# Scores and maxima of an attention kernel in 32-row tiles of TensorE, with the MLP run by token block between them

## The chip, the cores and the metric

The kernel runs on one core of one Trainium2 chip. The metric is the device time of one execution in microseconds. Before the change the median of 3 runs is 1124.44 us (1124.19 to 1124.58).

## The reference

One sequence of 2048 tokens, width 448, 16 heads of 28. Keys and values have one head, which all 16 query heads share. Attention and a two-layer MLP (hidden width 1792) both work on the normalized input, and both are added to it:

```python
xn = _layernorm(x, axis=-1)
# attention: one k and one v for all heads
q = (xn @ wq).reshape(B, S, H, Dh).transpose(0, 2, 1, 3)
k = xn @ wk
v = xn @ wv
scores = jnp.einsum("bhqd,bkd->bhqk", q, k) * (Dh ** -0.5)
o = jnp.einsum("bhqk,bkd->bhqd", _softmax(scores), v)
# result
x + o.transpose(0, 2, 1, 3).reshape(B, S, H * Dh) @ wo + jnp.maximum(xn @ w1, 0) @ w2
```

## The kernel before, in words

Matmuls that must be exact to float32 are made of single-pass float32r matmuls on parts: a value is split into a high part (rounded to float32r) and a low part (the rest), and high x high, high x low and low x high are summed in PSUM.

**Front.** x is loaded, normalized (`moments`, `rstd`, `normalized_x`), and transposed on PE (`transposed`, L222) into `xH`, `xL`, `xR`, which stay on chip. For each of four blocks of 512 tokens, `qkv_proj` (L252, L168, L173) makes four groups of columns: four heads each, with a part of k or v beside them. `qkv_out` splits each result (L235, L236) and stores high and low part to `qscr` in DRAM (L237).

**MLP.** It follows at once, before the attention. `tasks` runs over 7 parts of 256 hidden columns, and inside a part over the 4 token blocks. `mlp_up` makes two tiles of 11 matmuls (L168, L173), ACT applies the ReLU (L391), DVE makes the low part `hL` (L392). `mlp_down` makes four tiles of 6 matmuls (L404), which DVE adds into `acc` (L411). Each part's weights are loaded and split once (`split_part` on POOL, L147 and L148). Four of the 28 tasks also carry row maxima, 192 tiles in all.

**Attention.** A unit is one block of 512 queries and one group of four heads; there are 16 units, each with 16 blocks of 128 keys. `load_stack` puts four copies of the query parts over one another on 112 rows (high, low, high, low), and `kst` holds the keys in the same way (high, high, low, low), so one full-height matmul makes an exact score. `max_tile` (L350) makes a tile of scores with queries as rows, and DVE reduces it to row maxima (L354): 64 tiles a unit. When a unit is done, `max_all` and `max_rows` bring the negated maxima into two more rows of the query stack (L371, L373, L377), and `score` (L628) makes the scores with keys as rows, 114 rows high, with the maximum already taken off; ACT applies the exponential (L630) into a tile `p`. `pv` multiplies four heads' `p` tiles by the values, each in 32 columns of the array (L474), and a column of ones gives the denominators. Then `dens`, `recips`, `normalized` and the output projection (L529, L550) follow, and `finish` closes the last unit (L571 to L589).

**What sets the order.** Every engine runs its instructions in program order. In the attention a list written out by hand, `ORDER`, sets it: S is a score, M a maximum tile, V and a number so many PV blocks, F an output projection. PSUM has three pools: `psA` with 3 banks, `psM` with 4, `psO` with 1. All loads and stores from the middle of the program are issued from one queue, SP, in program order.

Of the kernel before, what the change touches and what calls it, by code (L numbers as in the profile page):

```python
# [15 lines left out]

@with_exitstack
def attention_plus_mlp(ctx: ExitStack, tc: tile.TileContext, x, wq, wk, wv, wo, w1, w2, out):
    nc = tc.nc
    P = 128
# [4 lines left out]
    NT = S // P  # L29
    QB = 512  # L30
    NQB = S // QB
    TPB = QB // P
    HG = 4
    NHG = H // HG
    NKB = S // P
# [4 lines left out]
    NPART = DFF // FP  # L40
# [5 lines left out]
    KQ = 4 * DH  # L46
    NU = NQB * NHG
    NA, NM = 3, 4
    assert DR == 64 and KQ + 2 <= P and HG * 32 == P and NPART * FP == DFF
# [5 lines left out]
    psA = ctx.enter_context(tc.tile_pool(name="psA", bufs=NA, space=PSUM))  # L55
    psM = ctx.enter_context(tc.tile_pool(name="psM", bufs=NM, space=PSUM))
    psO = ctx.enter_context(tc.tile_pool(name="psO", bufs=1, space=PSUM))


    acc = cst.tile([P, NT, D], F32, name="acc")  # L60
    xv = x.rearrange("(t p) d -> p t d", p=P)
    for t in range(TPB):
        (nc.scalar if t % 2 else nc.sync).dma_start(acc[:, t, :], xv[:, t, :])

    ident = cst.tile([P, P], F32, name="ident")
    make_identity(nc, ident)
    vtile = cst.tile([P, NKB, 32], F32, name="vtile")
    nc.gpsimd.memset(vtile, 1.0)
    ones2 = cst.tile([2, QB], F32, name="ones2")
    nc.gpsimd.memset(ones2, 1.0)  # L70
    eps_t = cst.tile([P, 1], F32, name="eps_t")
    nc.vector.memset(eps_t, EPS)
    warm = cst.tile([P, 1], F32, name="warm")

# [3 lines left out]
    kst = cst.tile([P, S], F32R, name="kst")  # L78
    qscr = dram.tile([NHG, 2, P, S], F32, name="qscr")
    rscr = dram.tile([NU, HG, QB], F32, name="rscr")  # L80
    stacks = ctx.enter_context(tc.tile_pool(name="stacks", bufs=3))


    mlp = ExitStack()
    spool = mlp.enter_context(tc.tile_pool(name="spool", bufs=2))
    wpool = mlp.enter_context(tc.tile_pool(name="wpool", bufs=2))
    xpool = mlp.enter_context(tc.tile_pool(name="xpool", bufs=1))
    hpool = mlp.enter_context(tc.tile_pool(name="hpool", bufs=2))
    proj_scope = ExitStack()
    npool = proj_scope.enter_context(tc.tile_pool(name="npool", bufs=1, side="right"))  # L90
# [13 lines left out]
    DHH = DH // 2  # L104
    MQ = HG * DH
    stg = spool.tile([P, 2048], F32, name="stg")
    s3 = stg[:, 0 : (DC + 1) * D].rearrange("p (c n) -> p c n", c=DC + 1)
    kvs = stg[:, (DC + 1) * D : (DC + 1) * (D + 2 * DH)].rearrange("p (c n) -> p c n", c=DC + 1)
# [4 lines left out]
    wqkv = wpool.tile([P, 2, 4, 512], F32R, name="w")  # L113
    w4 = wqkv.rearrange("p s c (g n) -> p s c g n", g=NHG)
    nc.gpsimd.memset(w4[:, :, :, :, MQ + DHH : P].bitcast(F32), 0.0)
    for t in range(TPB, NT):
        nc.sync.dma_start(acc[:, t, :], xv[:, t, :])

    def wqkv_parts(c, kv):
        src = (kvs if kv else s3)[:, c].rearrange("p (g n) -> p g n", g=NHG)  # L120
        cols = slice(MQ, MQ + DHH) if kv else slice(0, MQ)
        return src, w4[:, 0, c, :, cols], w4[:, 1, c, :, cols]
# [9 lines left out]
    parts = {}  # L132

    def load_part(p):
        f0 = p * FP
        g = spool.tile([P, 2048], F32, name="stg")
        chunks_in(g[:, 0:W1C].rearrange("p (c n) -> p c n", c=DC + 1), w1[:, f0 : f0 + FP])
        nc.sync.dma_start(
            g[:, W1C : W1C + W2C].rearrange("p (c n) -> p c n", c=FC),
            w2[f0 : f0 + FP].rearrange("(c p) n -> p c n", p=P),  # L140
        )
        return g

    def split_part(p, g):
        n = W1C + W2C
        wt = wpool.tile([P, 2, 2048], F32R, name="w")
        nc.gpsimd.tensor_scalar(wt[:, 0, 0:n], g[:, 0:n], 1.0, 0.0, op0=ALU.mult, op1=ALU.add)  # L147
        nc.gpsimd.tensor_tensor(wt[:, 1, 0:n], g[:, 0:n], wt[:, 0, 0:n].bitcast(F32), op=ALU.subtract)  # L148
        parts[p] = (
            wt[:, :, 0:W1C].rearrange("p s (c n) -> p s c n", c=DC + 1),  # L150
            wt[:, :, W1C:n].rearrange("p s (c n) -> p s c n", c=FC),
        )


    xH = xpool.tile([P, DC, S], F32R, name="xH")
    xL = xpool.tile([P, DC, S], F32R, name="xL")
    xR = xpool.tile([P, S], F32R, name="xR")
    kstF = kst.bitcast(F32)

    def proj(ps, lhs, cols, xs, between=None, middle=None):  # L160

        n = 0
        for ws, xm in (((0, 1), xH), ((0,), xL)):
            if middle and xm is xL:
                middle()
            for c in range(DC):
                for wi in ws:
                    nc.tensor.matmul(ps, lhs[:, wi, c, cols], xm[:, c, xs], start=n == 0, stop=False)  # L168
                    n += 1
                    if between and n % 4 == 0:  # L170
                        between()
        for wi in range(2):
            nc.tensor.matmul(ps, lhs[:, wi, DC, cols], xR[:, xs], start=False, stop=wi == 1)  # L173
# [3 lines left out]
    def moments(b):  # L177
        mv = small.tile([P, TPB, 2], F32, name="mv")
        for i in range(TPB):
            st = small.tile([P, 6], F32, name="st")  # L180
            nc.vector.bn_stats(st, acc[:, b * TPB + i, :])  # L181
            nc.vector.bn_aggr(mv[:, i, :], st)
# [3 lines left out]

# [11 lines left out]
    def normalized_x(b, on_act=(1, 3)):  # L198

        mv, rs, nb = stat.pop(b)  # L200
        xn = []
        for i in range(TPB):
            if i % 2 == 0:
                pair = hpool.tile([P, FC, QB], F32, name="hL" if i else "hH")
            n = pair[:, i % 2]
            a = acc[:, b * TPB + i, :]
# [10 lines left out]
    def transposed(b, xn, chunks=range(DC + 1), order=range(TPB)):  # L217
        xs = slice(b * QB, (b + 1) * QB)
        for c in chunks:
# [3 lines left out]
            if c < DC:  # L223
                nc.scalar.activation(xH[:, c, xs], pt, AF.Copy)
                nc.vector.tensor_tensor(xL[:, c, xs], pt, xH[:, c, xs].bitcast(F32), op=ALU.subtract)
            else:
                tmp = small.tile([P, QB], F32R, name="tmp")
                nc.scalar.activation(xR[0:DR, xs], pt[0:DR], AF.Copy)
                nc.scalar.activation(tmp[DR:P], pt[DR:P], AF.Copy)
                nc.vector.tensor_tensor(xR[DR:P, xs], pt[DR:P], tmp[DR:P].bitcast(F32), op=ALU.subtract)  # L230
# [7 lines left out]

    def qkv_proj(b, g, spare=False, middle=None):
        pq = psO.tile([P, QB], F32, name="o") if spare else psA.tile([P, QB], F32, name="a")  # L240
        proj(pq, wqkv, slice(g * P, (g + 1) * P), slice(b * QB, (b + 1) * QB), middle=middle)
        return pq

    def qkv_first(gs):

        pq = [psA.tile([P, QB], F32, name="a") for _ in gs]
        passes = [(0, xH, c) for c in range(DC)] + [(0, xL, c) for c in range(DC)] + [(0, None, DC)]
        passes += [(1, xH, c) for c in range(DC)] + [(1, None, DC)]
        for n, (wi, xm, c) in enumerate(passes):
            for k, g in enumerate(gs):  # L250
                rhs = xR[:, 0:QB] if xm is None else xm[:, c, 0:QB]
                nc.tensor.matmul(  # L252
                    pq[k], wqkv[:, wi, c, g * P : (g + 1) * P], rhs, start=n == 0, stop=n == len(passes) - 1
                )
        return pq

# [18 lines left out]


# [5 lines left out]
    g0 = load_part(0)  # L282
    g1 = load_part(1)
    pq = qkv_proj(0, 3, spare=True, middle=lambda: transposed(1, xn))
    qkv_out(0, 3, pq)
    for b in range(1, NQB):
# [10 lines left out]
        qkv_out(b, 2, qkv_proj(b, 2))  # L297
        if b == 2:
            split_part(0, g0)
        pq = qkv_proj(b, 3, middle=None if last else lambda: transposed(b + 1, xn))  # L300
        qkv_out(b, 3, pq)
    proj_scope.close()
    stacks2 = ctx.enter_context(tc.tile_pool(name="stacks2", bufs=2, side="right"))


    for g in range(2):
        for r in range(4):
            d0 = r * DH + g * DHH
            nc.sync.dma_start(kstF[d0 : d0 + DHH, :], qscr[g, r // 2, MQ : MQ + DHH])
    for b in range(NQB):  # L310
        nc.sync.dma_start(kstF[KQ : KQ + 2, b * QB : (b + 1) * QB], ones2)
    vT = []
    for s in range(2):
        t = stacks.tile([P, HG, QB], F32, name="qst")
        vT.append(t.rearrange("d j q -> d (j q)")[0:DH])
        for g in range(2):
            nc.sync.dma_start(vT[s][g * DHH : (g + 1) * DHH], qscr[2 + g, s, MQ : MQ + DHH])
    nc.gpsimd.tensor_tensor(vT[0], vT[0], vT[1], op=ALU.add)

    def v_rows():  # L320

        pv = psM.tile([P, QB], F32, name="m")
        for kb in range(NKB):
            nc.tensor.transpose(pv[:, kb * 32 : kb * 32 + DH], vT[0][:, kb * P : (kb + 1) * P], ident[0:DH, 0:DH])
        nc.vector.tensor_copy(vtile[:, :, 0:DH], pv.rearrange("p (i d) -> p i d", d=32)[:, :, 0:DH])


    qst, nmx, mx_todo = {}, {}, []
    units = [(b, g) for b in range(NQB) for g in range(NHG)]

    def load_stack(u):
        if u >= NU:
            return
        b, g = units[u]
# [353 lines left out]
```

## Time and profile before

| | |
|---|---|
| median of 3 runs | 1124.44 us |
| span of the profiled execution | 1122.0 us |
| PE busy | 1116.4 us, 99% |
| DVE busy | 791.9 us, 71% |
| ACT busy | 588.5 us, 52% |
| POOL busy | 115.9 us, 10% |
| instructions | 15424 |
| DMA, mean over the span | 41 GB/s |

The span runs from the first instruction of the profiled execution to the last. PE is TensorE's matmuls, PEld its weight loads, DVE VectorE, ACT ScalarE, POOL GpSimd, SP the queue that issues DMAs. A group's row reads: line, engine, operation, output<-input by the program's names, shapes, count, then busy time, mean ns of one, and idle time before it with what ended it. A matmul in float32 (L474) shows two instructions for one call. A matmul's own length includes its way through the array, so neighbours overlap: what one costs in a stream is the distance between starts.

### The profile page before, as it was taken

To read this page: it belongs to the slowest core of one execution; us is meant where nothing else is said; L and a number is where in the kernel's file an instruction comes from. 1 tells how busy PE (TensorE), PEld (TensorE's weight loads), DVE (VectorE), ACT (ScalarE), POOL (GpSimd) and SP (SyncE) were. 2 spreads that over 40 slices of the span, in tenths; PEclk is the share of its full clock that TensorE was granted. 3 is DMA by queue.
4 is the path that set the end of the run, shared out by engine and by line. 5 is a ranking of instruction groups with operands and counts; after the bars stand their busy time and mean duration, and the time that the engine had idled before them with its cause. 6 is when DMAs were issued, how large, how long until landed. Compare 5 with 4: busy or idle time off the path is not lost.

```text
span 1122.0 us, 15424 instructions
## 1 busy us (share of the span) xinstructions
PE 1116.4 (99%) x5900; PEld 743.6 (66%) x5900; DVE 791.9 (71%) x1383; ACT 588.5 (52%) x1173; POOL 115.9 (10%) x100
## 2 busy tenths in 40 slices
PE   9999999999999999999999999999999999999998
PEld 8888888888888755555656555556565555656555
DVE  7634337888888878778876878876877877777602
ACT  5511110011000467767866767766766777666894
POOL 3232022020200101010010101101011010010110
PEclk9999999999999999999999999999999999999999
DMA  7781610001000101011012020111101100000001
GB/s 242 259 175 39 144 36 1 1 1 37 1 1 1 30 1 44 12 33 44 15 30 59 11 52 2 44 24 37 43 18 44 33 12 11 18 11 10 11 11 41
DMA packets 34432, 45.95 MB, mean 41 GB/s; under 512 B 10056, under 2 KB 21000, under 8 KB 34192
## 3 DMA queue, kind: packets, MB, share of 16 engines
q1 hardware_dynamic: 34072, 44.52, 15.1%
q8 instruction: 46, 0.75, 0.3%
q10 hardware_dynamic: 288, 0.46, 0.1%
q14 instruction: 26, 0.21, 0.1%
HBM read 32.37 MB, written 12.18 MB: 40 GB/s over the span
## 4 chain that ended last, share of the span: by engine, by line
PE 99%; DVE 0%; DMA 0%; issue 0%; ACT 0%
PE a L628 22%; PE m L350 22%; PE o L474 21%; PE a L168 12%; PE a L404 9%; PE o L404 3%; PE a L173 3%; PE m L529 3%; PE m L628 1%; PE m L550 1%; PE a L252 1%; PE m L222 1%; DMA acc<-in_A_x 0%; PE a L588 0%; DVE st L181 0%; PE o L168 0%
## 5 line engine op out<-in xcount | busy, mean ns | idle before, releaser
L354 DVE TENSOR_REDUCE nmx<-m 128x1 f32<-128x512 f32 x1024 | 633.0, 681 | 151.5 <-PE m L350 151.1
L630 ACT ACTIVATE p<-a 128x512 f32<-128x512 f32 x974 | 495.0, 638 | 163.9 <-PE a L628 163.2
L350 PE MATMUL m<-kst,qst 112*128 112x512 f32 x1024 | 393.4, 400 | 0.0
L628 PE MATMUL a<-qst,kst 114*128 114x512 f32 x974 | 379.5, 413 | 0.0
L628 PEld LDWEIGHTS a<-qst,kst 114*128 114x128 f32 x974 | 182.9, 188 | 139.6 <-ACT p L630 63.6
L474 PE MATMUL o<-p,vtile 128*32 128x512 f32 x2048 | 236.3, 596 | 0.0
L350 PEld LDWEIGHTS m<-kst,qst 112*128 112x128 f32 x1024 | 193.5, 189 | 42.1 <-DVE nmx L354 12.5
L391 ACT ACTIVATE hH<-a 128x512 fp32r<-128x512 f32 x56 | 33.5, 599 | 266.0 <-PE a L173 143.0
L474 PEld LDWEIGHTS o<-p,vtile 128*32 128x32 f32 x2048 | 58.5, 109 | 127.2 <-issue 123.0
L168 PE MATMUL a<-xH,w 128*128 128x512 f32 x408 | 110.0, 392 | 0.0
L404 PE MATMUL a<-w,hH 128*128 128x448 f32 x336 | 96.0, 367 | 0.0
L392 DVE SCALAR_TENSOR_TENSOR hL<-a,hH 128x512 fp32r<-128x512 f32 x56 | 38.7, 692 | 69.7 <-ACT hH L391 69.7
L168 PEld LDWEIGHTS a<-xH,w 128*128 128x128 f32 x408 | 76.7, 188 | 15.8
L515 POOL TENSOR_TENSOR on<-rb,oS 128x512 f32<-128x512 f32 x15 | 19.3, 1289 | 643.9 <-DMA rb<-rscr 512.6
L404 PEld LDWEIGHTS a<-w,hH 128*128 128x128 f32 x336 | 63.6, 189 | 8.6
L168 PE MATMUL a<-xL,w 128*128 128x512 f32 x204 | 63.1, 392 | 0.0
L411 DVE TENSOR_TENSOR acc<-a,acc 128x448 f32<-128x448 f32 x84 | 51.8, 617 | 14.8 <-PE a L404 14.8
L404 PE MATMUL a<-w,hL 128*128 128x448 f32 x168 | 61.4, 365 | 0.0
L168 PEld LDWEIGHTS a<-xL,w 128*128 128x128 f32 x204 | 38.2, 188 | 8.2
L173 PE MATMUL a<-xR,w 128*128 128x512 f32 x136 | 41.9, 389 | 0.0
L404 PEld LDWEIGHTS a<-w,hL 128*128 128x128 f32 x168 | 31.6, 188 | 2.5
L404 PE MATMUL o<-w,hH 128*128 128x448 f32 x112 | 32.0, 367 | 0.0
(119 smaller groups left out, 536.9 us busy)
## 6 DMA issues: line engine op xcount, KB each, us to landing
qst<-qscr SPq DMA_DIRECT2D x64, 224.0 KB
qscr<-qs SPq DMA_DIRECT2D x16, 512.0 KB
rb<-rscr SPq DMA_DIRECT2D x60, 64.0 KB
out<-acc SPq DMA_DIRECT2D x16, 224.0 KB
acc<-in_A_x SPq DMA_DIRECT2D x14, 224.0 KB
stg<-in_B_w SPq DMA_DIRECT2D x7, 448.0 KB
stg<-in_B_w SPq DMA_DIRECT2D x7, 384.0 KB
d<-oS SPq DMA_DIRECT2D x60, 2.0 KB
```

The lines of the kernel that those rows point to most:

```text
L168: nc.tensor.matmul(ps, lhs[:, wi, c, cols], xm[:, c, xs], start=n == 0, stop=False)
L173: nc.tensor.matmul(ps, lhs[:, wi, DC, cols], xR[:, xs], start=False, stop=wi == 1)
L350: nc.tensor.matmul(pm, qst[u][0:KQ, j, s * P : (s + 1) * P], kst[0:KQ, k0 : k0 + QB], start=True, stop=True)
L354: nc.vector.tensor_reduce(nmx[u][:, n, h : h + 1], pm, axis=AX.X, op=ALU.max)
L391: nc.scalar.activation(hH[:, f], ph, AF.Relu)
L392: nc.vector.scalar_tensor_tensor(hL[:, f], ph, 0.0, hH[:, f].bitcast(F32), op0=ALU.max, op1=ALU.subtract)
L404: nc.tensor.matmul(py[:, 0:D], hm[:, f, i * P : (i + 1) * P], wd[:, wi, f, :], start=n == 0, stop=n == 3 * FC - 1)
L411: nc.vector.tensor_tensor(acc[:, t, :], py[:, 0:D], acc[:, t, :], op=ALU.add)
L474: nc.tensor.matmul(o_acc[u][32 * j : 32 * j + 32], vtile[:, kb, :], p, start=kb == 0, stop=kb == NKB - 1)
L529: nc.tensor.matmul(py[:, 0:D], om[:, i * P : (i + 1) * P], wm[:, g, :], start=n == 0, stop=n == 3 * NHG - 1)
L628: nc.tensor.matmul(pt, kst[0 : KQ + 2, kb * P : (kb + 1) * P], st, start=True, stop=True)
L630: nc.scalar.activation(p, pt, AF.Exp, scale=SCALE)
```

## The change: what it does

**Scores and maxima.** The stack of four copies goes. A head's q now lies in 32 rows of its own (28 used, and two for the negated maxima), four heads over one another; `kH` and `kL` hold the keys' high and low part four times, once in each 32 rows. A maximum tile is one matmul of 28 rows in one head's strip (`max_mm`, L735), of high parts alone. A score tile is three matmuls in its strip (`score_mm`, L772): high x high, high k x low q, and low k x high q with the two rows of maxima, 30 rows. The lines follow each other so that four strips have a matmul in turn, each strip with a PSUM bank of its own.

**MLP.** `tasks` now runs over token blocks, and inside a block over the 7 parts, and stands between the attention's work, so a part's weights are loaded and split once per block: 28 times. x is not kept on chip: `keep_x` stores each block's transposed parts to DRAM (L567), and `load_x` brings them back (L668) when the block's MLP comes. `acc` is loaded again by block.

**Order.** `ORDER` goes. A function `plan`, run when the program is built, makes the list from a table of durations and an account of 7 PSUM banks. It yields bursts ("rt": up to three matmuls in each of four strips), single matmuls of the MLP or the output projection ("fill"), PV blocks ("V") and side work. The list has 336 bursts three deep, 20 one deep, and 256 PV blocks; work on the full array, on 32-row strips and on 32-column strips follow one another in 960 runs. The MLP's first 40 up matmuls stand ahead of the first burst.

On PE in the attention, before the change: maxima (`kst,qst` into `m`) and scores (`qst,kst` into `a`) in turn, ahead of two PV blocks.

```order
L350 MATMUL m<-kst,qst 128x512 x2
L628 MATMUL a<-qst,kst 128x512 x2
L350 MATMUL m<-kst,qst 128x512
L628 MATMUL a<-qst,kst 128x512
L350 MATMUL m<-kst,qst 128x512
L628 MATMUL a<-qst,kst 128x512
L474 MATMUL o<-p,vtile 32x512 x8
L628 MATMUL a<-qst,kst 128x512 x2
```

The same place in the changed program, a burst and what follows it: L772 is a score's matmul, L735 a maximum, `b` a bank with its tile's number; the strip is not printed.

```order
L772 MATMUL b_1538<-q,kH 128x512
L772 MATMUL b_1540<-q,kH 128x512
L772 MATMUL b_1542<-q,kH 128x512
L735 MATMUL b_1544<-kH,q 128x512
...
L772 MATMUL b_1538<-q,kL 128x512
L772 MATMUL b_1540<-q,kL 128x512
L772 MATMUL b_1542<-q,kL 128x512
L735 MATMUL b_1562<-kH,q 128x512
L827 MATMUL o<-p,vtile 32x512 x4
L496 MATMUL b_1570<-xt,wu 128x512
```

Three scores have three matmuls each, the fourth strip three maxima; then one PV block (L827), one matmul of the MLP (L496), and the next burst.

On SP between the front and the MLP, before: the last store of q, then k (`kst`) and v (`qst`) from DRAM, and the next weights.

```order
L237 DMA qscr<-qs 128x2x512 x13
L309 DMA kst<-qscr 14x2048 x8
L311 DMA kst<-ones_86 2x512 x4
L317 DMA qst<-qscr 14x2048 x4
L98 DMA stg<-in_B_w 128x3x256
```

In the changed program at the same place: q and the last block of x go out, sixteen loads fill `kH` and `kL`, and x of block 0 (L668) follows them; then q of unit 0 and sixteen loads of v (L697).

```order
L574 DMA qscr<-qs 128x2x512 x4
L567 DMA xscr<-xt 128x3584
L662 DMA kH<-qscr 16x1x2048
L662 DMA kH<-qscr 12x1x2048
...
L662 DMA kL<-qscr 16x1x2048
L662 DMA kL<-qscr 12x1x2048
L668 DMA xt<-xscr 128x3584
L683 DMA q<-qscr 128x2x512
L697 DMA p<-qscr 16x1x512
```

The first matmul of the MLP has moved behind a load that comes last in this queue.

On POOL at the front of the MLP, in the changed program: the adds of v's halves (`p`), the output projection's weights (`wo`, `woH`, `woL`), and only then the split of the third part's weights (`wu`). Before, the output projection's weights came after the MLP.

```order
L704 TENSOR_TENSOR p<-p 28x512
L709 MEMSET wo 128x1792
L713 TENSOR_SCALAR woH<-wo 128x1792
L714 TENSOR_TENSOR woL<-wo,woH 128x1792
L470 TENSOR_SCALAR wu<-g_612 128x1024
L471 TENSOR_TENSOR wu<-g_612,wu 128x1024
```

The part's split waits for the output projection's weights now. The core of the diff:

```diff
+def plan(seed=0, slack=100, vmin=1, lead=2, pace0=0.20, pace1=1.00, k_at=9000, v_max=3, ns=3):
...
+            if sa and ma:
+                m_head = turn % HG
...
+                sh = [j for j in sa if j != mh][: ns]
+                rows = {j: ["S"] for j in sh}
...
+                lost = burst(rows, True)
+                if lost is not None and lost <= slack:
+                    best = rows
...
+    def keep_x(b):
+        nc.sync.dma_start(xscr[b], xT[b].bitcast(F32).rearrange("p c q -> p (c q)"))
...
+    kparts = ((0, HG * KV), (1, DH - HG * KV))
+    for s, dst in ((0, kH), (1, kL)):
+        for r in range(HG):
+            for g, n in kparts:
+                src = qscr[g, s].rearrange("(j d) q -> j d q", d=RB)[0 : n // KV, DH:RB]
+                d0 = r * RB + g * HG * KV
+                nc.sync.dma_start(dst.bitcast(F32)[d0 : d0 + n], src)
...
+    def load_x(b):
+        t = bpool.tile([P, NCH, QB], F32R, name="xt")
+        nc.sync.dma_start(t.bitcast(F32).rearrange("p c q -> p (c q)"), xscr[b])
+        xt2[b] = t
...
-        nc.tensor.matmul(
-            pm, qst[u][0:KQ, j, s * P : (s + 1) * P], kst[0:KQ, k0 : k0 + QB], start=True, stop=True
-        )
...
+        rows = slice(RB * r, RB * r + DH)
+        nc.tensor.matmul(
+            pm, qst[u][rows, 0, s * P : (s + 1) * P], kH[rows, h * QB : (h + 1) * QB], start=True, stop=True
+        )
...
-        nc.tensor.matmul(pt, kst[0 : KQ + 2, kb * P : (kb + 1) * P], st, start=True, stop=True)
...
+        k, s, m = ((kH, 0, DH), (kH, 1, DH), (kL, 0, DH + 2))[n]
+        rows = slice(RB * r, RB * r + m)
+        nc.tensor.matmul(pt_bank[r], k[rows, keys], qst[u][rows, s, :], start=n == 0, stop=n == 2)
...
-    tasks = [(p, b) for p in range(NPART) for b in range(NQB)]
...
+    tasks = [(b, p) for b in range(NQB) for p in range(NPART)]
...
+    order, *_ = plan()
+    for n, k in enumerate(order):
+        if k[0] == "rt":
+            for r, what, *a in k[1]:
+                (max_mm if what == "M" else score_mm)(r, *a)
```

More of the change, by code (lines that the diff above doesn't have):

```diff
@@ L77, in attention_plus_mlp @@
         nc.tensor.matmul(pw[:, 0:P], ident, ident, start=True, stop=True)
[L78 to L90, printed above, removed]
+    nc.gpsimd.memset(kL.bitcast(F32), 1.0)
     def chunks_in(dst, src, each=False):
@@ L310, in attention_plus_mlp @@
[L310 to L325, printed above, removed]
@@ new lines, in load_q @@
+        qst[u] = t
+    load_x(0)
+    load_q(0)
+    vparts = []
+    for b in range(NQB):
+        pair = []
+        for s in range(2):
+            t = ppool.tile([P, QB], F32, name="p")
+            for g, n in kparts:
+                src = qscr[2 + g, s].rearrange("(j d) q -> j d q", d=RB)[0 : n // KV, DH:RB, b * QB : (b + 1) * QB]
+                nc.sync.dma_start(t[g * HG * KV : g * HG * KV + n], src)
+            pair.append(t)
+        vparts.append(pair)
+    load_acc(0)
+    for u in range(1, 4):
+        load_q(u)
@@ new lines, in max_rows @@
+    def max_rows(u, b):
+        n = 2 * HG * TPB
+        pn = bank(b)
+        t = nm2.pop(u).rearrange("p j s i -> p (j s i)").bitcast(F32)
+        nc.tensor.transpose(pn[0:n, 0:P], t, ident)
+        rows = small.tile([n, P], F32, name="rows")
+        nc.scalar.activation(rows, pn[0:n, 0:P], AF.Copy)
+        dst = qst[u].bitcast(F32)
+        for j in range(HG):
+            r = RB * j + DH
+            nc.sync.dma_start(
+                dst[r : r + 2, 0].rearrange("s (i q) -> s i q", q=P), rows[j * 2 * TPB : (j + 1) * 2 * TPB]
+            )
@@ new lines, in down @@
+    def down(n, i):
+        b, p = tasks[n]
+        hH, hL = hid[n]
+        w = w_dn[n]
+        if p == 0 and i == 0 and b:
+            load_acc(b)
+        py = bank((yield))
+        k = 0
+        for f in range(FC):
+            for hm, wi in ((hH, 0), (hH, 1), (hL, 0)):
+                nc.tensor.matmul(
+                    py[:, 0:D], hm[:, f, i * P : (i + 1) * P], w[:, wi, f, :], start=k == 0, stop=k == 3 * FC - 1
+                )
+                k += 1
+                yield
+        nc.vector.tensor_tensor(acc[b][:, i, :], py[:, 0:D], acc[b][:, i, :], op=ALU.add)
+        if i == TPB - 1 and n + 2 < len(tasks):
+            next_dn(n + 2)
```

841 lines of the change are left out of this document (528 added, 313 removed).

## The prediction

> **What bounds the kernel now.** I read the page first, for the busy shares and the chain that ended last.
>
> ```profile
> span 1122.0 us, 15424 instructions
> ...
> PE 1116.4 (99%) x5900; PEld 743.6 (66%) x5900; DVE 791.9 (71%) x1383; ACT 588.5 (52%) x1173; POOL 115.9 (10%) x100
> ...
> PE 99%; DVE 0%; DMA 0%; issue 0%; ACT 0%
> PE a L628 22%; PE m L350 22%; PE o L474 21%; PE a L168 12%; PE a L404 9%; PE o L404 3%; PE a L173 3%; PE m L529 3%; PE m L628 1%; PE m L550 1%; PE a L252 1%; PE m L222 1%; DMA acc<-in_A_x 0%; PE a L588 0%; DVE st L181 0%; PE o L168 0%
> ...
> L354 DVE TENSOR_REDUCE nmx<-m 128x1 f32<-128x512 f32 x1024 | 633.0, 681 | 151.5 <-PE m L350 151.1
> ```
>
> PE is the chain. Scores (L628) and maxima (L350) are 45% of it, and the next engine, DVE, is at 71%, mostly with the 1024 maxima. So fewer PE passes pay in full until DVE is reached. A table of stages (busy us of PE, PEld, DVE, ACT, POOL; clock; DMA share; GB/s) shows whether this holds everywhere:
>
> ```profile
> 0.00:58.00 58.00, 56.02 (x295) 48.01 (x296) 39.99 (x99) 30.37 (x58) 17.96 (x35) 1.00 0.74 251
> 58.00:381.00 323.00, 323.00 (x1495) 278.99 (x1494) 221.04 (x370) 34.08 (x58) 41.42 (x13) 1.00 0.16 36
> 381.00:1112.60 731.60, 731.60 (x4093) 413.16 (x4091) 526.24 (x902) 523.30 (x1053) 55.43 (x48) 1.00 0.10 25
> 1112.60:1122.00 9.40, 5.74 (x27) 3.40 (x23) 4.64 (x13) 0.79 (x4) 1.09 (x4) 0.92 0.33 122
> ```
>
> It does: PE never rests after the start, and DMA matters only in the first 58 us, where its engines are already 74% busy. The timeline of PE gives the prices (start, length, what):
>
> ```profile
> 56.59 1.52 PE L168 MATMUL a<-xH,w 128*128 128x512 f32 x6
> ...
> 88.92 2.43 PE a L404 x12
> ...
> 93.87 2.04 PE a L168 x9
> ...
> 105.63 0.61 PE L173 MATMUL a<-xR,w 128*128 128x512 f32 x2
> 106.18 1.17 PE L324 MATMUL m<-ident,qst 28*128 28x28 f32 x16
> 107.28 0.67 PE L404 MATMUL a<-w,hH 128*128 128x448 f32 x2
> ...
> 381.66 0.39 PE L350 MATMUL m<-kst,qst 112*128 112x512 f32 x1
> ...
> 383.76 0.40 PE L628 MATMUL a<-qst,kst 114*128 114x512 f32 x1
> ...
> 385.69 0.39 PE L628 MATMUL a<-qst,kst 114*128 114x512 f32 x1
> 386.01 1.92 PE L474 MATMUL o<-p,vtile 128*32 128x512 f32 x16
> 387.87 0.50 PE L628 MATMUL a<-qst,kst 114*128 114x512 f32 x1
> ...
> 439.76 2.78 PE L474 MATMUL o<-p,vtile 128*32 128x512 f32 x24
> ...
> 1108.13 4.50 PE L474 MATMUL o<-p,vtile 128*32 128x512 f32 x40
> ```
>
> The MLP begins at 56.6. Its up matmul costs 2.04/9 = 0.227, its down matmul 2.43/12 = 0.2025. Scores and maxima alternate singly from 381.66 to 383.76, nine tiles: 0.234 each. A PV block is 8 instructions: (4.50 - 2.78)/2 = 0.86; its four 32-column tiles run side by side, for one after the other at even 0.2 an instruction would be 1.6. **A change of the array's shape** costs time: into L474 the gap is 0.32 instead of 0.234, and out of it two blocks take 1.86 instead of 1.72, so 0.09 and 0.14. The 28-row transposes L324 are 32-row work: they start 0.32 after the last L173 instead of 0.227, and 16 of them plus the way out take 1.10 where 16 x 0.063 (1.17 less one matmul's length of about 0.22, over 15) is 1.01: 0.09 each way. I take 0.105 a change.
>
> **The change, part by part.** PE's work from the first up matmul to the last PV block, counted from the instruction order:
>
> - Scores: 1024 tiles of three 28- or 30-row matmuls; maxima: 1024 of one; 4096 in all, four side by side. The list has 336 bursts three deep and 20 one deep: 1028 slots. No row shows four row tiles together. Below: 0.234, the price of one full matmul, as the column tiles of L474 behave. Above: four load-and-matmul pairs at the 0.063 of L324 is 0.252. I take 0.234, since L474 is the only row with four tiles in flight: 240.6 (above: 259). Before, the same two were 2048 x 0.234 = 479.
> - PV 256 x 0.86 = 220.2. Up 616 x 0.227 = 139.8, down 672 x 0.2025 = 136.1, output projection 171 x 0.203 = 34.7; the transposes of v and of the maxima 1.5. All unchanged.
> - Shape changes: the order has 959 of them (bursts, PV, full-array MLP in turn); before, 79 visits to L474, 158 changes. 959 x 0.105 = 100.7, against 16.6. This gives back a third of what the tiles save.
>
> Together 874. The same account for the old order gives 479 + 220 + 140 + 136 + 38 + 17 + 4 = 1034 where the trace has 1112.6 - 56.6 = 1056, so PE lost 22, or 2%, to waits. Now for waits. The bursts need three or four free banks at once, and DVE gets tighter:
>
> ```profile
> 443.01 7.27 DVE L354 TENSOR_REDUCE nmx<-m 128x1 f32<-128x512 f32 x12 [1.68 <-PE m L350]
> ...
> L392 DVE SCALAR_TENSOR_TENSOR hL<-a,hH 128x512 fp32r<-128x512 f32 x56 | 38.7, 692 | 69.7 <-ACT hH L391 69.7
> ...
> L411 DVE TENSOR_TENSOR acc<-a,acc 128x448 f32<-128x448 f32 x84 | 51.8, 617 | 14.8 <-PE a L404 14.8
> ```
>
> Back to back a maximum takes (7.27 - 0.68)/11 = 0.60, so 614 for all; with hL, the 112 adds and the 31 of the output projection about 736, and up to 104 more if hL and the adds wait as they did (69.7 + 14.8, and some 19 in the smaller groups of adds): 736 to 840 beside 874 of PE. ACT keeps its 588 or less and is no bound. I put the waits at 35 (4%); ends 18 (as before) and 85 (10%).
>
> **The start of the MLP is new.** x no longer stays on chip: each block goes to DRAM (L567, 1.83 MB) and comes back (L668), and the load of block 0 stands on SP behind 16 loads of k (L662).
>
> ```profile
> 30.00:40.00 10.00, 10.00 (x54) 8.50 (x53) 7.75 (x18) 5.88 (x11) 1.05 (x4) 1.00 1.00 363
> 60.00:70.00 10.00, 10.00 (x47) 8.63 (x46) 3.92 (x6) 1.80 (x3) 0.00 (x0) 1.00 0.92 130
> ...
> 58.59 3.83 SPq L309 DMA_DIRECT2D kst<-qscr  x8
> ...
> 0.74 3.34 DMA acc<-in_A_x
> ...
> 57.42 0.69 DVE L236 TENSOR_TENSOR qs<-a,qs 128x512 fp32r<-128x512 f32 x1 [1.80 <-ACT qs L235]
> ```
>
> Full DMA moves 363 GB/s; loading k (the only traffic after 60) 130. Three stores of x are 5.5 MB more within 20 to 58, where 260 GB/s already flow by the row below: 405 wanted, 363 to be had, 4.4 late. Then the last q (0.52 MB) and x of block 3 at 363: 6.5. Then k, now 1.83 MB where the eight L309 had half: 14.1 at 130. Then x back at 363: 5.1. First transfer from issue to landing took 3.34 with 0.23 MB in it, so 2.7 of latency. From 58.1, when the last q is ready (57.42 + 0.69), that is 90.9: **PE waits 34** where it waited for nothing. Ends: 21 (all at 363, nothing late) and 43 (x back at 130). The loads for blocks 1 to 3, and weights read four times instead of once (28 x 0.98 MB over some 900 us, 30 GB/s), come while bursts and PV fill PE and DMA stands at a share of 0.10: nothing.
>
> ```profile
> 20.00:58.00 38.00, 38.00 (x194) 32.09 (x193) 26.91 (x60) 20.94 (x38) 8.52 (x12) 1.00 0.74 260
> ...
> 79.06 1.79 POOL L147 TENSOR_SCALAR w<-stg 128x1920 fp32r<-128x1920 f32 x1
> 80.93 4.36 POOL L148 TENSOR_TENSOR w<-stg,w 128x1920 fp32r<-128x1920 f32 x1
> ...
> 74.47 4.61 POOL L318 TENSOR_TENSOR qst<-qst 28x2048 f32<-28x2048 f32 x1 [24.89 <-DMA qst<-qscr]
> ...
> L457 POOL MEMSET wo<- 128x1792 f32 x1 | 1.6, 1597 | 88.3 <-PE a L404 88.3
> ```
>
> POOL now splits weights per block and part, 28 x 6.2 = 172 where it was 43. Spread over the phase that hides behind PE, except at the front: four adds of v (4.6), a clear of 1.6, the landing of wo (3.3), its split (1.8 + 4.1, by size) and only then the third up part (6.2 x 1024/1920 = 3.3) follow v's landing: ready 19 later. The 16 loads of v take 0.48 each to issue (3.83/8), behind x, which puts the landing at about 96 and the part at 115. PE asks for it after 40 up matmuls (9.1), the pass for v, 24 down matmuls (4.9), four more ups and three bursts, some 17 after 91, at 108. PE waits 7; ends 0 and 15.
>
> The end is as it was: 9.4 from the last PV. **Sum:** 56.6 + 34 + 874 + 7 + 35 + 9.4 = 1016.0 of span. The profiled execution ran 1122.0 where the median is 1124.44, so 2.4 lie around the span: **1018 us**.
>
> Two rules of the Trainium skill stand against this. "TensorE: Matmul & The Clock Gate", section "Wait — 56ns, not 53.3ns?", puts about 62 ns of sequencer time on each matmul when hardware decoding is off. An estimate from it: 0.248 a slot and 1032 us. L324's 0.063 agrees, but cannot tell issue from weight load. "DMA: Bandwidth & Descriptors", section "Why a DMA increments its semaphore by 16 and not by 1", lets a transfer use only as many engines as divide the slowest dimension of both sides; this bears on the third rival.
>
> **Rivals.** (1) *Slower: the four tiles don't run beside each other.*
>
> ```profile
> L350 PEld LDWEIGHTS m<-kst,qst 112*128 112x128 f32 x1024 | 193.5, 189 | 42.1 <-DVE nmx L354 12.5
> ...
> L474 PEld LDWEIGHTS o<-p,vtile 128*32 128x32 f32 x2048 | 58.5, 109 | 127.2 <-issue 123.0
> ```
>
> A row tile loads 128 columns, 0.189 as in L350. One after the other that is 0.756 a slot: 1028 x 0.522 = 537 more, 1555 us. It decides from a slot of 0.234 + (1124.4 - 1018)/1028 = 0.338 on. Against it: L474's 2048 loads of 109 ns keep PEld busy for only 58.5, so loads of four column tiles do overlap. That the tiles are no tiles to the chip, and the change does not do what it says, is this rival too (four full matmuls, 0.94 a slot). (2) *DVE and banks bound the bursts*: 0.15 more in each of 336, 50 in all: 1068. For it: 840 of 874; against it: L350's weight loads, in the row above, waited for DVE only 12.5 in all. (3) *k comes on few engines*: the loads are pieces of 4 or 3 heads x 4 rows, so four engines or three. At 363/16 = 22.7 an engine four move 91 GB/s, 20 us; at 130/(16 x 0.92) = 8.8 they move 35, 52 us: up to 38 more, 1056. By that rule of "DMA: Bandwidth & Descriptors", this would happen; the 14-row loads of before do not show it.
>
> **How the numbers follow.** My sum holds 0.60 of the chance, its own ends 56.6 + 21 + 874 + 0 + 18 + 9.4 + 2.4 = 981 and, with all high ends, 1103; not all fall together, so 975 to 1065 for it. Rival 2 has 0.12, rival 3 has 0.13, rival 1 has 0.15. The range 975 to 1085 takes in the sum and rivals 2 and 3 and leaves out rival 1. About 0.2% (2.2 us) is what a measurement here can tell from nothing. Faster: 0.60 + 0.12 + 0.13 = 0.85, less 0.01 for the same; slower 0.15.
>
> **What would show it.** Right: scores and maxima start four within one slot of 0.23 to 0.25, a gap of 0.09 to 0.14 at each change of shape, PE idle for about 34 before the first up matmul, a short wait for POOL at the third part, PE's chain long and DVE above 80% in the middle. Wrong: slots over 0.3; k still landing after 100; waits on DVE or banks above 50 in all; shape changes between 32 rows and the full array at 0.2 or more, each 0.1 of which adds 96.

## The result, and the profile after

The changed kernel takes 1130.01 us (median of 4 runs, 1129.53 to 1130.51) beside 1124.46 for the kernel before in the same runs. The ratio is 1.0051, with a 95% interval of 1.0036 to 1.0065: half a per cent slower, where 1018 was forecast with a range of 975 to 1085. 112 us of expected gain are missing.

The page after: span, busy shares, the chain of work that ended last by engine and by line, and the group of the maxima. A q behind an engine's name stands for its sequencer.

```profile
span 1127.8 us, 20444 instructions
...
PE 1053.8 (93%) x7948; PEld 547.3 (49%) x7948; DVE 803.5 (71%) x1383; ACT 608.8 (54%) x1173; POOL 255.3 (23%) x201
...
PE 81%; DMA 6%; DVE 3%; SPq 2%; ACT 1%; POOL 1%; issue 1%; DVEq 0%; ACTq 0%; POOLq 0%
PE o L827 22%; PE b L772 19%; PE b L809 13%; PE b L496 11%; PE b L735 7%; PE b L866 4%; PE b L501 3%; DVE nmx L738 2%; DMA d<-oS 2%; DMA q<-qscr 2%; DMA kL<-qscr 1%; ACT p L775 1%; DMA kH<-qscr 1%; SPq L837 1%; DMA wo<-in_A_wo 1%
...
L738 DVE TENSOR_REDUCE nmx<-b 128x1 f32<-128x512 f32 x1024 | 642.9, 684 | 138.7 <-PE b L735 100.9
```

Scores (L772) and maxima (L735) fell from 45% of the chain to 26%, so the tiles do what they were made for, and yet the span did not shrink. PE is still the chain, at 81%; DMA is on it now. The stages (busy us of PE, PEld, DVE, ACT, POOL; granted clock as a share of full speed; DMA share; GB/s):

```profile
0.00:58.00 58.00, 52.59 (x268) 43.73 (x269) 38.02 (x96) 28.77 (x56) 26.34 (x41) 0.97 0.88 301
58.00:100.00 42.00, 4.85 (x22) 3.69 (x20) 2.08 (x3) 1.69 (x3) 0.00 (x0) 0.60 0.69 238
100.00:200.00 100.00, 86.56 (x439) 59.88 (x441) 70.96 (x120) 15.84 (x29) 47.96 (x29) 0.90 0.33 95
200.00:400.00 200.00, 196.52 (x1554) 90.73 (x1554) 161.80 (x271) 122.08 (x236) 41.82 (x29) 0.97 0.16 49
```

From 58 to 100 PE does next to nothing. From 200 to 400 it is busy at 98% and DVE at 81%. A busy PE says little here, since the length of a matmul includes its way through the array and the pauses around a change of shape are short. They show only in the distance between starts. The timeline of PE at one burst, with a PV block ahead of it and an MLP matmul behind (start, length, what):

```profile
298.59 1.06 PE L827 MATMUL o<-p,vtile 128*32 128x512 f32 x8
299.59 0.49 PE L772 MATMUL b<-q,kH 28*128 28x512 f32 x1
299.59 0.49 PE L735 MATMUL b<-kH,q 28*128 28x512 f32 x1
299.60 0.49 PE L772 MATMUL b<-q,kH 28*128 28x512 f32 x2
299.93 0.38 PE L735 MATMUL b<-kH,q 28*128 28x512 f32 x1
299.93 0.39 PE L772 MATMUL b<-q,kH 28*128 28x512 f32 x3
300.15 0.39 PE L735 MATMUL b<-kH,q 28*128 28x512 f32 x1
300.16 0.40 PE L772 MATMUL b<-q,kL 30*128 30x512 f32 x3
300.48 0.47 PE L809 MATMUL b<-wd,hL 128*128 128x448 f32 x1
```

Four strips start within 0.01 us of each other. The second slot begins 0.34 after the first, the third 0.22 after the second (medians of the 320 bursts of twelve matmuls: 0.337 and 0.232), and the next shape 0.32 after the last of these matmuls, 0.09 more than a slot. So a change of shape is paid **twice**: a pause of 0.09 where one shape ends, and 0.105 more for the first matmul of the next. The same stood in the profile of before, in the rows that follow the 439.76 of the prediction:

```profile
442.47 0.50 PE L350 MATMUL m<-kst,qst 112*128 112x512 f32 x1
442.81 0.39 PE L628 MATMUL a<-qst,kst 114*128 114x512 f32 x1
443.04 0.40 PE L350 MATMUL m<-kst,qst 112*128 112x512 f32 x1
```

The first full-height matmul behind the PV blocks holds PE for 0.34, the next for 0.23.

**An account of the phase.** From the first up matmul (102.7) to the last of PV (1117.9) lie 1015.2. Of these, 771 are the work at the prediction's prices, with 0.232 for a slot in place of 0.234. Of 959 changes, 704 lead into a burst or into full-height work, at 0.09 + 0.105, about 0.20; 255 lead into PV, whose first pass is only 0.044 longer: 0.136. That is 141 + 35 = 175. What is left, 69, I call waits. The same account is made of each run below.

### The profile page after: what moved, and what is told of

Same layout as the page of the kernel before. It is cut to its first block, busy times and chain, and to the rows that moved or that the text cites. A ratio compares the mean times of both kernels' runs of the same rounds, so it can differ in the third digit from the quotient of the medians.

```text
span 1127.8 us, 20444 instructions
## 1 busy us (share of the span) xinstructions
PE 1053.8 (93%) x7948; PEld 547.3 (49%) x7948; DVE 803.5 (71%) x1383; ACT 608.8 (54%) x1173; POOL 255.3 (23%) x201
## 4 chain that ended last, share of the span: by engine, by line
PE 81%; DMA 6%; DVE 3%; SPq 2%; ACT 1%; POOL 1%; issue 1%; DVEq 0%; ACTq 0%; POOLq 0%
PE o L827 22%; PE b L772 19%; PE b L809 13%; PE b L496 11%; PE b L735 7%; PE b L866 4%; PE b L501 3%; DVE nmx L738 2%; DMA d<-oS 2%; DMA q<-qscr 2%; DMA kL<-qscr 1%; ACT p L775 1%; DMA kH<-qscr 1%; SPq L837 1%; DMA wo<-in_A_wo 1%
## 5 line engine op out<-in xcount | busy, mean ns | idle before, releaser
L738 DVE TENSOR_REDUCE nmx<-b 128x1 f32<-128x512 f32 x1024 | 642.9, 684 | 138.7 <-PE b L735 100.9
L775 ACT ACTIVATE p<-b 128x512 f32<-128x512 f32 x1024 | 537.5, 599 | 321.9 <-PE b L772 229.1
L735 PE MATMUL b<-kH,q 28*128 28x512 f32 x1024 | 324.2, 439 | 5.8 <-DVE nmx L738 2.7
L827 PE MATMUL o<-p,vtile 128*32 128x512 f32 x2048 | 277.6, 615 | 0.0
L772 PE MATMUL b<-q,kH 28*128 28x512 f32 x2048 | 262.2, 450 | 2.2 <-DVE hL L795 1.0
L496 PE MATMUL b<-xt,wu 128*128 128x512 f32 x504 | 162.6, 434 | 54.4 <-issue 39.9
L735 PEld LDWEIGHTS b<-kH,q 28*128 28x128 f32 x1024 | 163.2, 185 | 45.8 <-issue 17.6
L772 PEld LDWEIGHTS b<-q,kH 28*128 28x128 f32 x2048 | 117.8, 184 | 112.4 <-issue 77.5
L496 PEld LDWEIGHTS b<-xt,wu 128*128 128x128 f32 x504 | 92.9, 195 | 150.3 <-issue 107.8
L809 PE MATMUL b<-wd,hH 128*128 128x448 f32 x448 | 142.9, 389 | 2.3 <-DVE hL L795 1.1
L772 PE MATMUL b<-q,kL 30*128 30x512 f32 x1024 | 141.2, 396 | 0.2 <-DMA q<-rows 0.2
L827 PEld LDWEIGHTS o<-p,vtile 128*32 128x32 f32 x2048 | 40.6, 108 | 84.0 <-issue 80.4
L772 PEld LDWEIGHTS b<-q,kL 30*128 30x128 f32 x1024 | 71.9, 186 | 4.4 <-DMA q<-rows 0.5
```

Of the source, the lines that this page charges most:

```text
L496: nc.tensor.matmul(ps, lhs(wi, c), xt[:, base + c], start=n == 0, stop=False)
L735: nc.tensor.matmul(pm, qst[u][rows, 0, s * P : (s + 1) * P], kH[rows, h * QB : (h + 1) * QB], start=True, stop=True)
L738: nc.vector.tensor_reduce(nmx[u][:, r, s, h : h + 1], pm, axis=AX.X, op=ALU.max)
L772: nc.tensor.matmul(pt_bank[r], k[rows, keys], qst[u][rows, s, :], start=n == 0, stop=n == 2)
L775: nc.scalar.activation(p, pt_bank.pop(r), AF.Exp, scale=SCALE)
L809: nc.tensor.matmul(py[:, 0:D], hm[:, f, i * P : (i + 1) * P], w[:, wi, f, :], start=k == 0, stop=k == 3 * FC - 1)
```

## Experiments

The theory after this reading: a change of shape costs 0.2, not 0.105; the front costs 12 more than forecast; the rest are waits. The rivals: DVE or the banks bind; or the changes are cheap and something else fills the phase. Times stand beside 1124.3 to 1124.5 for the kernel before. Each is one run, unless a range is given; four runs of one version spread by 1 to 5 us, as the ranges show.

**The price of a change, by itself.** Ahead of each of the 168 up and down tiles of the MLP stands one more matmul of 512 columns, into the same bank, which the next one overwrites. In one kernel it has full height, so the order of shapes stays; in the other it has 28 rows, which makes 257 more changes. The line of the one and of the other:

```diff
+        nc.tensor.matmul(ph, kL[0:128, 0:P], kL[0:128, 0:QB], start=True, stop=True)
...
+        nc.tensor.matmul(ph, kL[0:28, 0:P], kL[0:28, 0:QB], start=True, stop=True)
```

> One extra full-height matmul of 512 columns ahead of each of the 168 up and down tiles, into the tile's own bank, which the tile's first matmul then overwrites. No change of shape is added (960 in the order, as in the changed kernel). Both theories: PE is the bound, so 168 x 0.23 = 39 us more, 1169. If DVE or the banks are the bound (rival), PE has slack and less than half of it shows: under 1150.

> The same extra matmul, but 28 rows high: 257 more changes of shape in the order than with the full-height one. Theory 1 (a change costs about 0.2: 0.09 on the way out and 0.105 more before the second matmul of the new shape): 257 x 0.197 = 51 us over the run with the full-height matmul, 1220. Theory of the prediction (0.105 a change): 27 over it, 1196. Rival (banks and DVE are the bound): less than 10 over it.

Measured 1162.47 and 1208.58. The 168 full-height matmuls cost 32.5, and 28 rows instead of 128, with the same columns, 46.1 more: 0.179 a change. At 0.105 it would have been 27. The theory's price stands, a little below 0.2.

**Is DVE the bound?** The maxima are taken over 256 of the 512 keys, the other half is left out of them.

```diff
-        nc.vector.tensor_reduce(nmx[u][:, r, s, h : h + 1], pm, axis=AX.X, op=ALU.max)
+        nc.vector.tensor_reduce(nmx[u][:, r, s, h : h + 1], pm[:, 0 : QB // 2], axis=AX.X, op=ALU.max)
```

> Each maximum is taken over 256 of the 512 keys in its tile, so the row maxima cover half of the keys: DVE has some 270 us less work, PE and the order are the same. Rival (DVE and the banks it holds are the bound of the bursts): 50 us or more faster, below 1080. Theory 1 (changes of shape on PE): within 15 us of 1130, since PE's work stays.

Measured 1115.86. The group of the maxima in this run:

```profile
L738 DVE TENSOR_REDUCE nmx<-b 128x1 f32<-128x256 f32 x1024 | 371.7, 417 | 317.6 <-PE b L735 211.9
```

DVE lost 271 us of work and the kernel 14. DVE doesn't bind this order; it makes some 14 of the 69 (its account leaves 55). Some 8 of the 14 show in the bursts of twelve: from first start to last they take 0.600 on average here, where the changed kernel's take 0.626.

**The front.** First, x and q of unit 0 are loaded ahead of k:

```diff
+    load_x(0)
+    load_q(0)
...
     for s, dst in ((0, kH), (1, kL)):
```

> The loads of x of block 0 and of q of unit 0 are put ahead of the sixteen loads of k. If the load of x is what the front loses (theory A): the MLP starts at about 79 instead of 102.7 and the total falls by some 20 us, to 1110. If the queue behind it is (theory B: k, then v, then the output projection's weights and the POOL split behind them, which end at 132): PE starts early and stands still later, and the total stays within 4 us of 1130.

Measured 1119.29, 10.7 less and between the two theories, though the MLP started 24 earlier, at 78.7. PE then stood 14 at the transposes of v, and 12 at the third part, whose split still stood behind `woL` on POOL. So in the second version x goes first, k comes once from DRAM in four loads and is copied on chip to the three other strips, and the output projection's weights are loaded and split when they are needed:

```diff
+    for s, dst in ((0, kH), (1, kL)):
+        for g, n in kparts:
+            src = qscr[g, s].rearrange("(j d) q -> j d q", d=RB)[0 : n // KV, DH:RB]
+            nc.sync.dma_start(dst.bitcast(F32)[g * HG * KV : g * HG * KV + n], src)
...
+    for r in range(1, HG):
+        for dst in (kH, kL):
+            nc.sync.dma_start(dst.bitcast(F32)[r * RB : r * RB + DH], dst.bitcast(F32)[0:DH])
...
+        if u == 0:
+            load_wo()
```

> The order as in the changed kernel, the front mended: x of block 0 first, k loaded once from DRAM (4 loads) and copied on chip into the other three strips (6 copies of 28 rows), and the output projection's weights split when the first unit's denominators come. Theory B (the queue on SP and POOL behind x is what the front loses): the MLP starts at 79, no wait over 3 us before the third part, 30 us faster than the changed kernel, 1100. If few engines were not the cause of the slow loads of k: k lands as late as before (100), and the gain stays under 15.

Measured 1101.94. The timeline of its PE:

```profile
79.07 3.86 PE L496 MATMUL b<-xt,wu 128*128 128x512 f32 x9 [16.84 <-issue]
...
94.11 0.79 PE L737 MATMUL b<-kH,q 28*128 28x512 f32 x1 [3.69 <-DMA kH<-kH]
```

PE waits 17 instead of 40 for x, 7 for the copies of k in three waits (3.7, 1.8 and 1.9), and no more for v or the weights. Theory B held, but for the first of these three, which is over 3 us. The phase is close to what it was: 1011.2, with 65 of waits. Four runs of the same kernel:

> The changed kernel with the new front alone, once more and timed in rounds: 1102, as in the single look (1101.94), which is 2% below the kernel before. If the single look was a lucky one, the interval says so.

1103.82 (1102.12 to 1105.13), a ratio of 0.9817 to the kernel before, with an interval of 0.9802 to 0.9831. It beats the kernel before by 1.8% and the changed one by 2.3%.

**Fewer changes.** If a change costs 0.2, an order with fewer should gain. `plan` was made to put at least so many MLP matmuls or PV blocks together: 748 changes (the edit below, alone and with the new front) and 603 (`fmin=3, vmin=3`, with SW left at 100 and the line of `left` as it was). Here `fmin` and `vmin` are the least numbers of MLP matmuls and of PV blocks, SW is the plan's price of a change, `slack` the wait that it allows a burst, and the other two set how early the attention starts and how fast the MLP goes.

```diff
+def plan(fmin=1, seed=0, slack=100, ...
-    SLOT, MM, MD, VB, SW = 232, 228, 204, 858, 100
+    SLOT, MM, MD, VB, SW = 232, 228, 204, 858, 200
-            left = mlp and min(tasks[k[1]][0] for k in mlp[:3]) <= b and proj[0][1][0] == "O"
+            left = mlp and min(tasks[k[1]][0] for k in mlp[:3]) <= b
+                for _ in range(fmin - 1):
+                    w = "cur" if cur else fill_start()
+                    if w and (cur or (w != "O" and done < allowed)) and (cur or any(not y for y in busy)):
+                        fill_one()
-    order, *_ = plan()
+    order, *_ = plan(fmin=8, slack=200, pace0=0.2, k_at=5000)
```

> Only the order of the list changes: work on the full array comes in runs of at least 8 matmuls and a burst may wait 200 ns instead of 100 for its banks; 748 changes of shape instead of 960, the same matmuls. Theory 1 (a change costs 0.18, as the extra matmuls showed): 212 x 0.18 = 38 us faster than the changed kernel, 1092. Rival (banks and evacuations are the bound, changes of shape only fill their waits): within 8 us of 1130.

> PV comes three blocks at a time where it can, and full-array work at least three matmuls at a time: 603 changes of shape instead of 960. Theory 1 alone: 357 x 0.18 = 64 us faster, 1066. If the bursts' waits for banks and probabilities take the place of the changes (rival), most of it is eaten up: 1100 to 1130, with PE's waits on DVE and ACT in the profile grown by as much.

> The order of the run with 748 changes of shape and the mended front together. Theories 1 and B: 1130 - 38 - 30 = 1062, some 5% faster than the kernel before. If either falls: over 1085.

Measured 1125.23, 1168.14, and 1108.79 (median of 4 runs, 1105.95 to 1109.88; ratio 0.9865, interval 0.9849 to 0.9882). Theory 1 missed all three: with 748 changes only 5 were gained, as the rival had it, with 603 the kernel lost 38, beyond the rival too, and on the new front the order lost 5. With 603 the changes cost some 62 less and the waits are some 100 more (phase 1053.8); why they grew so much was not tried. The account of the order with 748: 1010.2 = 771 + 134 + 105. The changes became 41 cheaper, and waits rose by 36. Its bursts of twelve took 0.784 on average from first start to last, where the changed kernel's take 0.626 and one without any wait 0.582. What PEld waited for in it (line, waited for, total, times, longest):

```profile
PEld b L776 <- DVE nmx L742: 106.7, 136, 1.3
...
PEld b L739 <- DVE nmx L742: 75.4, 162, 2.3
```

That pointed to DVE. The next run took it at its word: the same order with the halved maxima.

> The order with 748 changes of shape, and maxima over 256 of the 512 keys of each tile (so the output is off where the maximum lies in the other half; the time of DVE is what is wanted). With the full maxima this order took 1125.2 and stood 101.7 in waits, 76.4 of them ahead of bursts. Theory A: those waits are for DVE, which has become the second bound of this phase; with its maxima half as long they fall to about 45 or less, and the run comes to 1060 to 1080, the gain that fewer changes should have brought. Rival B: the waits come from the order itself (banks held by scores for ACT, tiles too few), and halving the maxima gives here only what it gave to the changed kernel, 14: about 1111.

Measured 1105.29, 20 less: between the two theories, nearer to the rival's 1111. A burst took 0.730, and 86 of waits were left. Its timeline shows one kind that DVE has no part in (PE and PEld):

```profile
700.55 0.65 PE L776 MATMUL b<-q,kH 28*128 28x512 f32 x3
...
700.88 0.54 PE L776 MATMUL b<-q,kH 28*128 28x512 f32 x3
...
701.20 0.18 PEld L739 LDWEIGHTS b<-kH,q 28*128 28x128 f32 x1 [0.20 <-ACT p L779]
...
701.20 0.51 PE L776 MATMUL b<-q,kL 30*128 30x512 f32 x3
```

The third slot starts 0.32 after the second instead of 0.232: the third maximum of the fourth strip waits for a bank that ACT's exponential is about to free, and the strips behind it in the queue wait with it. So both ways out of the banks were halved: the exponential covers 256 of 512 queries, and the tiles `p` are fixed buffers whose other half is set to zero once.

```diff
+    pbuf = [ppool.tile([P, QB], F32, name=f"p{i}") for i in range(P_BUFS)]
...
-            nc.scalar.activation(p, pt_bank.pop(r), AF.Exp, scale=SCALE)
+            nc.scalar.activation(p[:, 0 : QB // 2], pt_bank.pop(r)[:, 0 : QB // 2], AF.Exp, scale=SCALE)
```

> The order with 748 changes, with both ways out of the score banks halved: maxima over 256 of 512 keys on DVE, and the exponential over 256 of 512 queries on ACT (the other half of each tile of exponentials keeps zeros from the start; the output is off by that). With the maxima alone halved it took 1105.3, and a burst of twelve matmuls took 0.730 from its first start to its last, where the changed kernel needs 0.626 and a burst without any wait 0.582. Theory A: bursts wait for banks, whoever empties them, ACT now more than DVE; with both halved a burst falls to about 0.60 and the run to 1060 to 1070. Rival B: the waits are in the order of the list, a bank being asked for before anything could have emptied it: bursts stay above 0.68, 1090 or more.

> The changed kernel in its own order (960 changes), with both ways out of the score banks halved in the same way. Theory A (each change of shape has its price of about 0.2, and the banks alone hid it in the order with fewer): this run takes 35 to 45 more than the order with 748 changes under the same halving, and itself about 1110, little under the 1115.9 with the maxima alone halved, as here few waits are left. Rival B (fewer changes bring nothing in themselves): the two are within 15 of each other.

Measured 1067.89 and 1109.79, both as theory A had them (the burst a little longer than its 0.60). Two slots of a burst in the first of these:

```profile
703.80 0.50 PE L784 MATMUL b<-q,kH 28*128 28x512 f32 x3
...
704.14 0.39 PE L784 MATMUL b<-q,kH 28*128 28x512 f32 x3
...
704.36 0.40 PE L784 MATMUL b<-q,kL 30*128 30x512 f32 x2
```

0.34 and 0.22, nothing waits; a burst takes 0.632. Both accounts leave 48 of waits, and the runs are 41.9 apart for 212 changes: 0.2 each. The price is confirmed in place, and so is what hid it: with full exponentials and maxima the bursts of this order wait for ACT and DVE to empty the seven banks, and that takes back most of what fewer changes give. Halving shortens both the work of the two engines and the time that one bank is held; the runs don't tell which of the two binds. The view of waits would have misled once more. Of this run it says:

```profile
PEld b L784 <- DVE nmx L750: 99.1, 120, 1.4
```

Nearly what this order had with full maxima, although its bursts hardly wait any more. It is idle time of weight loads, and 97% of it lies beside a PV block that keeps PE busy.

**A truer table.** The last kernel has the new front and, of the plan, only the price of a change set to 200.

> The front of the second version (x ahead of k, k loaded once and copied on chip, output projection weights later) with one number of the plan's table set to what the runs showed: 200 ns for a change of shape where it had 100. The list then has 967 changes, as many as before, but its account of time is nearer to the chip's. Theory A: the waits ahead of bursts come from DVE and PE being near each other in work, whatever the account says: within 8 of the 1101.9 of that front alone. Rival B: they come from an account that runs ahead of the chip, so the bank that a burst wants is not yet free: the waits fall by 20 or more, 1080 or less.

Measured 1118.2 (median of 4 runs, 1115.75 to 1120.72), a ratio of 0.9938 (0.9918 to 0.9958) to the kernel before, and 14 more than the same front with the old table. Neither theory had this. With 966 changes it has 7 more than the other list, and its account 82 of waits instead of 65. So two lists with the same work and nearly as many changes differ by 14 us, and a better price in the table did not make the better list. The bursts of twelve take 0.646 on average instead of 0.624, some 7 of the 14; where the rest goes, and why the bursts wait longer, was not tried.

## Why the prediction was wrong, step by step

The miss of 112 is, by the account: changes of shape 75, waits in the phase 27, the front 12, and the work 2 less.

**The step that failed: "I take 0.105 a change."** It was mis-sized. 959 changes cost 175, not 100.7. The prediction took 0.09 into L474 and 0.14 over two PV blocks and out of them, both rightly read as distances between starts, but it never looked at the first matmul behind the blocks, whose 0.34 stood one row below those that it used. The way into the row strips it took from transposes of 28 columns and not from matmuls of 512. By the right price, the 158 changes before the change would also have cost some 10 more than the account gave them, about half of the 22 that it put down to waits; that was the sign. It had named the test itself, 0.2 or more at a change and 96 more for each 0.1, but gave this case no chance: as the forecast was 1018, 0.2 alone would have led to about 1109, beyond the range.

"TensorEngine Tiling (Array Packing)" of the Trainium skill says, in its section "Key Properties", that a change of tiling mode drains the engine, and gives no price. The trace agrees as to the 0.09 at the end of a shape; the 0.105 of the first matmul behind it goes beyond that.

**The four tiles side by side: right.** 0.232 a slot; the first rival, 1555, did not come, nor did the 0.248 of the prediction's estimate. The work is 771 where 773 was forecast.

**The front: mechanism right, size 12 off.** Forecast 90.6, measured 102.7. The last QKV matmul starts at 62.2, where the MLP's first had started at 56.6 before. In part this is PE's wait in the front for ACT to write the transposed x (the view of waits from 10 to 64: line, waited for, total, times, longest):

```profile
PE a L496 <- ACT xt L558: 3.0, 2, 2.8
```

Then the third rival happened. SP's queue, and four stages of the DMA:

```profile
64.64 1.31 SPq L567 DMA_DIRECT2D xscr<-xt  x1
66.47 7.58 SPq L662 DMA_DIRECT2D kH<-qscr  x8
74.77 9.43 SPq L662 DMA_DIRECT2D kL<-qscr  x8
84.77 0.35 SPq L668 DMA_DIRECT2D xt<-xscr  x1
```

```profile
75.00:80.00 5.00, 0.00 (x0) 0.00 (x0) 0.00 (x0) 0.00 (x0) 0.00 (x0) 0.50 0.25 107
80.00:85.00 5.00, 0.00 (x0) 0.00 (x0) 0.00 (x0) 0.00 (x0) 0.00 (x0) 0.50 0.24 93
...
95.00:100.00 5.00, 0.00 (x0) 0.00 (x0) 0.00 (x0) 0.00 (x0) 0.00 (x0) 0.50 0.36 110
100.00:103.00 3.00, 0.28 (x1) 0.31 (x2) 0.00 (x0) 0.00 (x0) 0.00 (x0) 0.50 0.18 71
```

A share of 0.25 is four of sixteen engines, at 93 to 107 GB/s in all: near the rival's 91, not the 35 of its dear end. By the rule that the prediction named from "DMA: Bandwidth & Descriptors" of the Trainium skill, loads of 4 heads x 4 rows would use four engines; the trace agrees. x was issued behind all sixteen loads, at 84.8, and then had to share the engines with them: by their packets, k's transfers (8 KB each) run from 72 to 97, 25 where 14.1 was forecast and 20 was the rival's price, and those of x (14 KB) from 86 to 102, 16 where 5.1 was forecast; from 100 on the share is down to 0.18. The first up matmul comes right behind:

```profile
102.72 4.18 PE L496 MATMUL b<-xt,wu 128*128 128x512 f32 x9 [39.88 <-issue]
```

**POOL at the third part: right, its size in part by luck.** PE waited 8.4, where 7 was forecast (a row of PE, then two of POOL):

```profile
131.80 0.79 PE L496 MATMUL b<-xt,wu 128*128 128x512 f32 x1 [8.37 <-POOL wu L470]
...
126.78 3.96 POOL L714 TENSOR_TENSOR woL<-wo,woH 128x1792 fp32r<-128x1792 f32 x1
130.70 1.05 POOL L470 TENSOR_SCALAR wu<-g 128x1024 fp32r<-128x1024 f32 x1
```

Both ends came 15 to 17 later than forecast, PE's asking (123 instead of 108) and the first split of the weights (131.75, where the whole part was to be ready at 115), so the distance between them fits better than either does.

**Waits in the phase: 69, where 35 and the 7 of POOL were forecast.** Halved maxima take 14 of them away, halved exponentials on top 7 more, and some 48 stay. About 9 of these are the wait for POOL, and 17 to 20 are the clock, which the prediction did not have at all (below). The cause of the last 20 or so was not shown; as halving does not empty the banks at once, some of them may still be waits for banks. The second rival (50 more, the bursts bound by DVE and banks) came with the 14 that halved maxima take away and is not what made this kernel slow, but it is what stands behind the price of the changes: waits took back 36 of 41 in the order with fewer.

**The end and what lies around the span: right** (9.8 and 1.7, where 9.4 and 2.4 were forecast).

## What to carry to other kernels

Price a switch of mode from the distance between starts on both sides of it, and over the first instruction behind it as well, before multiplying it by a thousand. Where a change trades passes for switches and leaves two engines close to each other, an edit that relieves the first engine gains only what the second leaves room for; a trial run that leaves out half of the second's work tells how much that is. And time waited by weight loads is no time lost by PE: read the distances between matmuls.

## What the runs showed of the hardware

**Half clock after short waits.** Before the change the granted clock was full until the last 2 us. In the changed kernel it fell to 0.5 six times within the phase, for 3.4, 6.8 or 10.2 us, 41 in all, and the first 4.4 us of the phase still ran at half clock behind the wait for x; at half speed about 20 of these are lost, an estimate that leaves out the 4 in which PE stood waiting for POOL. One such place (stages as above):

```profile
247.00:250.60 3.60, 3.11 (x16) 1.60 (x12) 1.68 (x5) 1.58 (x3) 0.00 (x0) 1.00 0.04 6
250.60:254.00 3.40, 2.56 (x14) 1.18 (x14) 3.40 (x8) 0.97 (x3) 0.00 (x0) 0.98 0.19 37
254.00:264.20 10.20, 10.20 (x54) 3.80 (x52) 4.86 (x9) 3.75 (x8) 3.17 (x3) 0.50 0.04 14
```

PE was busy for 2.56 of 3.40 us, the longest wait that reaches into them was 0.81, and the next 10.2 ran at half clock. Four of the other five falls begin within a single wait of 2 to 8 us or just behind it. "TensorE: Matmul & The Clock Gate" of the Trainium skill tells, in its section "A second HAM failure mode: psum-queue depth-cycling", of a kernel whose micro-idles between groups of matmuls, as it cycles through PSUM banks, make the clock swing. The trace agrees at this place, where 0.81 was the longest such idle. So a wait for a bank seems to be paid again in clock; that is read from the order of events, and no run here tested it. The run with 603 changes had a mean granted clock of 0.949 where the changed kernel has 0.962.

**Row strips.** Four matmuls of 28 or 30 rows and 512 columns, each with 128 columns of weights, take 0.232 together, as long as one of full height.
